# Weight loads in alternating thirds, a split first q load, and values cast on ScalarE, in a sketched-attention plus ReGLU kernel

## The chip, the core and the metric

The kernel runs on one core of a Trainium2 chip. The metric is the device time of one execution in microseconds (us); lower is better. A core has five engines that run side by side, each in its own program order: TensorE (PE, matrix multiplies; its weight loads are listed as PEld), VectorE (DVE), ScalarE (ACT), GpSimd (POOL) and SyncE (SP, which only issues DMAs here). An engine whose next instruction waits does nothing else meanwhile.

## The reference, cut to what matters

```python
# q, k, v: (4 batches, 4 heads, 1088 tokens, 32) float32;  S1, S2: (8, 32)
def phi(x):                       # 64 features of a token
    a = einsum('rd,bhsd->bhsr', S1, x)
    b = einsum('rd,bhsd->bhsr', S2, x)
    return einsum('bhsi,bhsj->bhsij', a, b).reshape(..., 64)
q_p, k_p = phi(q), phi(k)
kv = einsum('bhsf,bhsd->bhfd', k_p, v)
z = sum(k_p, axis=2)
attn = einsum('bhsf,bhfd->bhsd', q_p, kv) / (einsum('bhsf,bhf->bhs', q_p, z) + 1e-6)
x = attn.transpose(0, 2, 1, 3).reshape(4352, 128)
out = (maximum(x @ w_gate, 0) * (x @ w_val)) @ w_out     # w_gate, w_val: 128 x 1536; w_out: 1536 x 128
```

## The kernel before

**Order of work.** The whole program is unrolled, and its order is worked out in Python while it is built. Every piece of work is a `Task` with an engine, an estimated length (`occ`) and latency (`lat`), tasks that it depends on (`deps`), tasks that must merely have started (`after`) and an earliest time (`at`). `set_due` (L55) gives each task a due time, going back from the due times of the feed-forward units by latency and a slack of 200 ns for each step. `run` (L84) then puts the tasks in order: on each engine it takes, among those that can start first (within 30 ns), the one due soonest. The times in `land` (L322) are estimates of when each load has landed; a consumer is not placed earlier. The result is only an order: on the chip each engine goes through its own list, and a wrong estimate becomes a wait in which everything behind it on that engine waits too.

**Attention.** A batch has 1088 = 64 x 17 tokens, 17 columns (`c`) of 64, the first CA = 9 in partitions 0 to 63 and the other CB = 8 in partitions 64 to 127. For each batch the keys go through: two transposes of `k_sb` on DVE (L405), sketches on PE (L415), transposes back (L427), the outer product `kp` on POOL (L301; for batch 0 partly on DVE), the sum for z (L474, L486, L491, L499, ending in `wst`), and `kp` times `v_sb` on PE (L513) into `kv_bd` (L528). The queries go in groups: columns 0, 1, 2 to 3 and 4 to 7 (of each half) of batch 0, then columns 0 to 7 of batches 1, 2 and 3, then the last column of all batches. A group goes: transpose of `q_sb` (L588), PE (L612), transpose back (L627), the denominator (`bw`, `dn`, `rd`, `an`; L637 to L654), the outer product `qp` (L301; POOL from the third group on), a transposition (PE L671 and ACT L712 for batch 0; a transposing DMA on SP, L701, for batches 1 to 3), PE (L678), and an ACT cast into `xT` (L720).

**Feed-forward.** 102 units, each of 512 columns of work: gate product (PE L747 with `wg`), value product (PE L747 with `wv`), ReLU (ACT L758), their product `ht` (DVE L767) and four matmuls with `wo` that accumulate the output (PE L778). The 12 blocks `j` of 128 of the hidden dimension are split among units: a unit of the first two groups covers 4 blocks, of the third 2, then 1. After a group's units ACT copies the result out (L795) and SP stores it (L801). Up to 5 PSUM banks hold gate and value products, 14 buffers hold `ht`.

**Loads.** SP starts with S1 and the two halves of batch 0's k, then the whole of batch 0's q (L246). POOL issues the loads that cast float32 to float16 on the way: v of batch 0 (L239 and L240, two DMAs), then `wg`, `wv` and `wo` (L367, one DMA each), then v of batches 1 to 3 (two DMAs each). `fills` (L291) are four small memsets of a batch's tiles, on POOL for batches 1 to 3; the first of them stands ahead of v's load. `gate` (L393) is a POOL memset of one element of `k_sb` of batch 1: SP's load of that tile, and all of SP's loads behind it (k1, q1, k2, q2, k3, q3; L390 and L391), wait for it. Until the first unit PE runs multiplies of zeros (L824) in its idle time.

Of the kernel before, what the change touches and what calls it, by code (L numbers as in the profile page):

```python
# [9 lines left out]
FP32 = mybir.dt.float32  # L10
# [28 lines left out]
class Plan:  # L39
# [4 lines left out]
    def __init__(self, free, a_max, f_max, n_banks):  # L44
        self.tasks = []
        self.free = dict(free)
        self.a_max, self.f_max, self.n_banks = a_max, f_max, n_banks
        self.sem = 45.0

    def add(self, *args, **kw):  # L50
        t = Task(*args, **kw)
        self.tasks.append(t)
        return t

    def set_due(self, slack):  # L55
        after = {}
        for t in self.tasks:
            for d in t.deps + t.after:
                after.setdefault(id(d), []).append(t)
        order, seen = [], set()  # L60

        def visit(t):
            stack = [(t, iter(after.get(id(t), ())))]
            seen.add(id(t))
            while stack:
                top, it = stack[-1]
                for n in it:
                    if id(n) not in seen:
                        seen.add(id(n))
                        stack.append((n, iter(after.get(id(n), ()))))  # L70
                        break
                else:
                    order.append(top)
                    stack.pop()

        for t in self.tasks:
            if id(t) not in seen:
                visit(t)
        for t in order:
            for n in after.get(id(t), ()):  # L80
                s = slack if n.kind != "f" or t.kind != "f" else 0.0
                t.due = min(t.due, n.due - t.lat - s)

    def run(self, first_f):  # L84
# [97 lines left out]
def kernel(  # L182
# [12 lines left out]
    nc = tc.nc  # L195

    B, H, S, D = q.shape
# [4 lines left out]
    NJ = DF // 128  # L202
    T = 64
    C = S // T
    CA = (C + 1) // 2
    CB = C - CA
    NG = 10
    NH = 14
    assert (B, H, D, R, C) == (4, 4, 32, 8, 17)

    ctx.enter_context(tc.manual_schedule())
# [11 lines left out]
    k_sb = [const.tile([128, 2, C * D], FP32, name=f"k_sb{b}") for b in range(B)]  # L223
    q_sb = [const.tile([128, 2, (C + 1) * D], FP32, name=f"q_sb{b}") for b in range(B)]
    v_sb = [const.tile([128, H, CA * D], FP16, name=f"v_sb{b}") for b in range(B)]
    wg = const.tile([DM, NJ, 128], FP16, name="wg")
    wv = const.tile([DM, NJ, 128], FP16, name="wv")
    wo = const.tile([128, NJ, DM], FP16, name="wo")

    def load_pairs(eng, dst, src, b, hp=None):  # L230
        x = src[b].rearrange("(x y) (t c) d -> (y t) x (c d)", y=2, c=C)
        if hp is None:
            eng.dma_start(out=dst[:, :, 0:C * D], in_=x)
        else:
            eng.dma_start(out=dst[:, hp, 0:C * D], in_=x[:, hp])

    def load_v(eng, dst, b):
        x = v[b].rearrange("h (t c) d -> t h (c d)", c=C)
        eng.dma_start(out=dst[0:T], in_=x[:, :, 0:CA * D])  # L239
        eng.dma_start(out=dst[T:128, :, 0:CB * D], in_=x[:, :, CA * D:])  # L240
# [2 lines left out]
    nc.scalar.dma_start(out=s16[R:2 * R], in_=S2[:, None, :].to_broadcast([R, 4, D]))  # L243
    load_pairs(nc.sync, k_sb[0], k, 0, 0)
    load_pairs(nc.sync, k_sb[0], k, 0, 1)
    load_pairs(nc.sync, q_sb[0], q, 0)  # L246

    zero = const.tile([128, 128], FP16, name="zero")
    nc.vector.memset(zero, 0.0)  # L249
# [40 lines left out]

    def fills(eng, b):  # L291
        eng.memset(wst[b], 0.0)
        eng.memset(v_sb[b][T:128, :, CB * D:], 0.0)
        eng.memset(kt[b][:, :, C], 0.0)
        eng.memset(kv_bd[b], 0.0)

# [8 lines left out]
            op=ALU.mult,  # L305
        )

    T0, STEP, T_GATE, T_DT = 12500.0, 830.0, 12500.0, 2500.0
    P = Plan(free={"PE": 1200.0, "ACT": 3100.0, "DVE": 3600.0, "POOL": 3000.0, "SP": 20000.0},
             a_max=3, f_max=5, n_banks=7)  # L310

    def act(n):
        return dict(occ=50 + 0.835 * n, lat=175 + 0.835 * n)
# [4 lines left out]
    def pool(n):  # L318
        return dict(occ=70 + 1.86 * n, lat=120 + 1.86 * n)

    T_S = 4000.0
    land = dict(k00=4200.0, k01=4850.0, q0=6700.0, v0=8700.0, wg=10500.0, wv=13000.0, wo=16500.0,  # L322
                k1=17500.0, v1=20000.0, q1=20500.0, k2=22500.0, v2=23000.0, q2=24500.0, k3=26500.0,
                v3=26000.0, q3=28500.0)


    def e_st(t):
# [38 lines left out]
    def e_load(dst, src):  # L366
        return lambda t: nc.gpsimd.dma_start(out=dst, in_=src)  # L367

    l_v0 = P.add("ld_v0", "POOL", 1350, 1350, emit=lambda t: load_v(nc.gpsimd, v_sb[0], 0))
    l_g = P.add("ld_wg", "POOL", 740, 740, deps=[l_v0],  # L370
                emit=e_load(wg, moe_w_gate.rearrange("m (j f) -> m j f", j=NJ)))
    l_v = P.add("ld_wv", "POOL", 560, 560, deps=[l_g],
                emit=e_load(wv, moe_w_val.rearrange("m (j f) -> m j f", j=NJ)))
    l_o = P.add("ld_wo", "POOL", 1050, 1050, deps=[l_v],
                emit=e_load(wo, moe_w_out.rearrange("(j f) m -> f j m", f=128)))
    l_v_sb = [l_v0]
    l_v0.after += t_fill[:1]
    for f in t_fill[1:]:
        f.after.append(l_o)
    prev = l_o  # L380
    for b in range(1, B):
        prev = P.add(f"ld_v{b}", "POOL", 1350, 1350, deps=[prev, t_fill[b - 1]],
                     emit=lambda t, b=b: load_v(nc.gpsimd, v_sb[b], b), at=10000.0 + 3000.0 * b)
        prev.due = T0 - 1000.0 + 5000.0 * b
        l_v_sb.append(prev)

    def e_gate(t):
        nc.gpsimd.memset(k_sb[1][0:1, 0, 0:1], 0.0)
        for b in range(1, B):
            load_pairs(nc.sync, k_sb[b], k, b)  # L390
            load_pairs(nc.sync, q_sb[b], q, b)  # L391

    P.add("gate", "POOL", 70, 100, emit=e_gate, at=T_GATE).due = T_GATE  # L393


    class Keys:
# [2 lines left out]
    kk = []  # L399
    for b in range(B):  # L400
        K = Keys()
        kk.append(K)

        def ke_t1(t, b, hp):
# [100 lines left out]
        K.wst = P.add(f"k{b}wst", "DVE", **dve(32), deps=[K.w, t_w0[b]], frees=[K.z],  # L505
                      emit=lambda t, b=b, z=K.z: ke_wst(t, b, z))

        K.v = [P.add(f"v{b}", "POOL", 1, 1, deps=[l_v_sb[b]], at=land[f"v{b}"])]

        def ke_kv(t, b, lo, hi, m):  # L510
            for c in range(lo, hi):
# [55 lines left out]
    for i, (bs, c0, n, r, o0) in enumerate(groups):  # L567
        G = Group()
        gg.append(G)
        G.bs, G.c0, G.n = bs, c0, n  # L570
        X = 4 * n
        rest = len(bs) > 1
        early = i < 2
        turned = not rest and bs[0] > 0
# [22 lines left out]
        for hp in range(2) if turned else (None,):  # L597
            cost = dict(occ=560, lat=640) if rest else dve((2 if turned else 4) * n * 32, 85)
            t1.append(P.add(f"q{i}t1{hp}", "DVE", **cost, deps=free,
                            at=max(land[f"q{b}"] for b in bs),  # L600
                            emit=lambda t, G=G, hp=hp: qe_t1(t, G, hp)))

        def qe_ab(t, G):
# [89 lines left out]
        for c in range(0, n, 4):  # L693
            p = Part()
            G.parts.append(p)
            p.G, p.n, p.c0, p.col = G, min(n, 4), c, col
            col += p.n * 128
            need = phi if n <= 4 else phi[2 * (c // 4):2 * (c // 4) + 2]
            if turned:
                def qe_dt(t, G=G, c=c):  # L700
                    nc.sync.dma_start_transpose(  # L701
                        out=G.pt[:, 2 * c:2 * c + 8],
                        in_=G.qp[:, 4 * c:4 * c + 16].rearrange("s x f -> s (x f)"))

                tre = P.add(f"q{i}dt{c}", "SP", T_DT, T_DT + 1500, deps=need, after=[last_dt],
                            emit=qe_dt)
                last_dt = tre
            else:
                tr = P.add(f"q{i}tr", "PE", 58 * 2 * p.n, 58 * 2 * p.n + 170, deps=need, banks=1,
                           emit=lambda t, G=G, p=p: qe_tr(t, G, p.c0, p.n))  # L710
                tre = P.add(f"q{i}tre", "ACT", **act(256 * p.n), deps=[tr], frees=[tr],
                            emit=lambda t, G=G, f=tr, p=p: nc.scalar.copy(  # L712
                                out=G.pt[:, 2 * p.c0:2 * p.c0 + 2 * p.n].rearrange(
                                    "f x t -> f (x t)"),
                                in_=ps[:, f.bank].bitcast(FP16)[:, 0:2 * p.n * 128]))
            num = P.add(f"q{i}num{c}", "PE", 110 * p.n, 110 * p.n + 170, banks=1,
                        deps=[tre] + [kk[b].kvc for b in bs],
                        emit=lambda t, G=G, p=p: qe_num(t, G, p.c0, p.n))
            p.x = P.add(f"q{i}x{c}", "ACT", **act(128 * p.n), deps=[num], frees=[num],
                        emit=lambda t, p=p, f=num: nc.scalar.copy(  # L720
                            out=xT[:, p.col:p.col + p.n * 128], in_=ps[:, f.bank, 0:p.n * 128]))
            before.setdefault(id(r), []).append(p.x)
# [8 lines left out]
    for gi, p in enumerate(p for G in gg for p in G.parts):  # L731
# [3 lines left out]
        for i in range(NJ // per):  # L735
# [9 lines left out]
            def e_mm(t, w, p=p, js=js, W=W):  # L745
                for y, j in enumerate(js):
# [1 line left out]
                                     xT[:, p.col:p.col + W], start=True, stop=True)  # L748

            g = P.add(f"g{u}", "PE", 218, 218 + 170, deps=[p.x], banks=1, kind="f",  # L750
                      emit=lambda t, f=e_mm: f(t, wg), at=land["wg"])
            vv = P.add(f"v{u}", "PE", 218, 218 + 170, deps=[p.x, g], banks=1, kind="f",
                       emit=lambda t, f=e_mm: f(t, wv), at=land["wv"])
            g.due, vv.due = due, due + 220

            def e_relu(t, U, g):
# [53 lines left out]
                           emit=lambda t, G=G, p=p: e_evict(t, G, p))  # L810
        last_evict.due = outs[-1].due + 400

    P.set_due(200.0)
    order = P.run(T0)


# [42 lines left out]
```

## Time and profile before

| What | Value |
|---|---|
| median of 3 runs | 110.31 us (110.23 to 110.49) |
| the profiled execution | 110.49 us |
| its span, first to last instruction | 108.7 us |
| granted TensorE clock over the span | 0.993 |
| PE matmuls, busy | L747 with `wg` 35.6 us, with `wv` 36.6 us, L778 39.1 us |
| ACT, ReLU (L758) | 57.2 us, 602 ns each |
| DVE, product `ht` (L767) | 63.9 us, 676 ns each |
| HBM read and written | 9.05 MB, 2.23 MB |

Busy times of pipelined matmuls overlap, so their sum is more than the time that they hold PE; back to back, a unit's three products start 0.22 us apart each. In the timelines below, a bracket at a line's end gives the engine's idle time just before it and what ended it.

### The profile page before, as it was taken

The numbers are of one execution on the slowest core, as the hardware profiler recorded it, in microseconds if no ns is written. First come the engines' busy times: TensorE is split into PE (matmuls) and PEld (weight loads), VectorE is DVE, ScalarE is ACT, GpSimd is POOL, SyncE is SP. The second block draws the span as 40 slices with busy tenths as digits, with TensorE's granted clock in tenths as the row PEclk, the third lists the DMA queues.
The fourth block names the chain that finished last, engine by engine and source line by source line (L and its number), as shares of the span: only waits on it lengthen the run. The fifth ranks groups of instructions, "written<-read, shape, count | busy, mean of one in ns | idle before, by whom it ended". The sixth has DMA issues, their size and how long they took to land.

```text
span 108.7 us, 3081 instructions
## 1 busy us (share of the span) xinstructions
PE 99.8 (92%) x1175; PEld 66.7 (61%) x1175; DVE 91.6 (84%) x199; ACT 72.2 (66%) x140; POOL 51.1 (47%) x84
## 2 busy tenths in 40 slices
PE   6999978599999999999999999999999999999930
PEld 6778767187657554656576556565774666568710
DVE  4659973899999998999999799799995999889820
ACT  4330469168597619666978495499767989989910
POOL 6979898089829719503294088025925000000000
PEclk9999999999999999999999999999999999999997
DMA  1999999999912582100045440000471400400302
GB/s 38 319 184 158 156 221 300 309 310 311 222 31 48 103 99 54 42 0 6 0 96 113 86 96 3 0 0 11 106 148 30 103 0 0 99 1 6 82 14 48
DMA packets 14559, 10.75 MB, mean 99 GB/s; under 512 B 8657, under 2 KB 11345, under 8 KB 14545
## 3 DMA queue, kind: packets, MB, share of 16 engines
q1 hardware_dynamic: 10328, 8.20, 29.3%
q0 software_dynamic: 4016, 2.29, 15.5%
q8 instruction: 9, 0.15, 0.5%
q10 hardware_dynamic: 200, 0.07, 0.3%
q14 instruction: 6, 0.04, 0.1%
HBM read 9.05 MB, written 2.23 MB: 104 GB/s over the span
## 4 chain that ended last, share of the span: by engine, by line
PE 68%; DMA 16%; DVE 6%; POOL 3%; ACT 1%; SPq 1%; issue 1%; DVEq 1%
PE ps L747 37%; PE ps L778 18%; DMA k_sb<-in_k_dram 7%; DMA q_sb<-in_q_dram 5%; DMA pt<-qp 4%; PE ps L678 3%; PE ps L612 3%; PE ps L415 2%; POOL qp L301 2%; PE ps L474 2%; DVE kp L301 1%; ACT xT L720 1%; PE ps L513 1%; DVE abq L627 1%; DVE qt L588 1%
## 5 line engine op out<-in xcount | busy, mean ns | idle before, releaser
L758 ACT ACTIVATE g_sb<-ps 128x512 f16<-128x512 f32 x102 | 57.2, 602 | 16.3 <-PE ps L747 14.7
L767 DVE TENSOR_TENSOR ht<-g_sb,ps 128x512 f16<-128x512 f16 x102 | 63.9, 676 | 4.2 <-ACT g_sb L758 1.5
L778 PEld LDWEIGHTS <-ht 128*128 128x128 f16 x408 | 29.5, 98 | 17.8 <-DVE ht L767 4.1
L778 PE MATMUL ps<-wo,ht 128*128 128x128 f16 x408 | 39.1, 219 | 0.4 <-DVE ht L767 0.4
L747 PE MATMUL ps<-xT,wv 128*128 128x512 f16 (+2 forms) x132 | 36.6, 331 | 0.8 <-DMA wv<-in_moe_w_val_dram 0.8
L747 PE MATMUL ps<-xT,wg 128*128 128x512 f16 (+2 forms) x132 | 35.6, 330 | 0.6 <-ACT xT L720 0.5
L301 POOL TENSOR_TENSOR kp<-abk 128x640 f16<-128x640 f32 (+1 forms) x14 | 16.3, 1193 | 8.2 <-DVE abk L427 8.2
L301 POOL TENSOR_TENSOR qp<-an,abq 128x512 f16<-128x512 f32 x16 | 16.7, 1070 | 0.5
L747 PEld LDWEIGHTS <-wv 128*128 128x128 f16 x132 | 11.4, 98 | 4.6 <-issue 1.4
L747 PEld LDWEIGHTS <-wg 128*128 128x128 f16 x132 | 11.7, 98 | 3.7 <-issue 1.7
L637 POOL TENSOR_TENSOR bw<-abq 128x128 f32<-128x128 f32 (+1 forms) x9 | 3.8, 424 | 14.0 <-DVE abq L627 13.7
L720 ACT CAST xT<-ps 128x512 f16<-128x512 f32 (+2 forms) x11 | 5.4, 488 | 5.4 <-PE ps L678 5.4
L824 PE MATMUL ps<-zero 128*128 128x128 f16 x84 | 7.7, 250 | 1.1 <-DVE zero L249 1.1
L405 DVE STREAM_TRANSPOSE kt<-k_sb 128x544 f32<-128x544 f32 x8 | 5.6, 726 | 2.9 <-DMA k_sb<-in_k_dram 2.9
L654 POOL TENSOR_TENSOR an<-abq,rd 128x256 f32<-128x256 f32 (+2 forms) x6 | 2.9, 480 | 9.4 <-DVE rd L651 9.3
L824 PEld LDWEIGHTS <-zero 128*128 128x128 f16 x84 | 6.1, 113 | 1.7 <-DVE zero L249 1.1
L627 DVE STREAM_TRANSPOSE abq<-ps 128x512 f32<-128x512 f32 (+2 forms) x11 | 6.3, 577 | 0.8 <-PE ps L612 0.7
L795 ACT ACTIVATE o_sb<-ps 128x512 f32<-128x512 f32 (+2 forms) x11 | 5.5, 501 | 2.0 <-PE ps L778 1.9
L415 PE MATMUL ps<-kt,sk 64*64 64x288 f32 x64 | 5.4, 425 | 1.6 <-DVE kt L405 1.6
L678 PE MATMUL ps<-pt,kv_bd 128*128 128x512 f16 (+2 forms) x20 | 5.1, 337 | 0.3 <-DMA pt<-qp 0.2
L612 PE MATMUL ps<-qt,wst 64*64 64x256 f32 (+3 forms) x112 | 5.1, 303 | 0.0
L427 DVE STREAM_TRANSPOSE abk<-ps 128x320 f32<-128x320 f32 (+1 forms) x8 | 3.4, 460 | 1.9 <-PE ps L415 1.8
(75 smaller groups left out, 64.4 us busy)
## 6 DMA issues: line engine op xcount, KB each, us to landing
q_sb<-in_q_dram SPq DMA_DIRECT2D x4, 544.0 KB, 8.8
out_dram<-o_sb SPq DMA_DIRECT2D x14, 128.0 KB, 2.3
k_sb<-in_k_dram SPq DMA_DIRECT2D x3, 544.0 KB, 8.6
v_sb<-in_v_dram POOLq DMA_DIRECT2D x4, 144.0 KB, 8.6
k_sb<-in_k_dram SPq DMA_DIRECT2D x2, 272.0 KB, 2.7
v_sb<-in_v_dram POOLq DMA_DIRECT2D x4, 128.0 KB, 10.1
wg<-in_moe_w_gate_dram POOLq DMA_DIRECT2D x1, 384.0 KB, 7.2
wv<-in_moe_w_val_dram POOLq DMA_DIRECT2D x1, 384.0 KB, 8.5
```

What stands on the lines that cost most here:

```text
L301: eng.tensor_tensor(out=dst.rearrange("s x (i j) -> s x i j", i=R), in0=a[:, :, :, None].to_broadcast([128, n, R, R]), in1=b[:, :, None, : ...
L405: nc.vector.transpose(kt[b][:, hp, 0:C].rearrange("p c t -> p (c t)"), k_sb[b][:, hp])
L415: nc.tensor.matmul(ps[64 * st:64 * st + 64, first.bank + h2, 0:CA * 32], sk[r, 64 * hp:64 * hp + 64], kt[b][r, hp, CA * st:CA * st + CA].r ...
L612: nc.tensor.matmul(o, wst[G.bs[0]][r, hp].rearrange("p a f -> p (a f)"), G.qt[r, hp, st], start=True, stop=True, skip_group_check=True)
L627: nc.vector.transpose(G.ab[:, lo:hi].rearrange("p x h f -> p h x f"), ps[:, f.bank:f.bank + 2, lo * 32:hi * 32].rearrange("p h (x t) -> p ...
L678: nc.tensor.matmul(o, kv_bd[G.bs[0]][:, 2 * hp:2 * hp + 2].rearrange("f a d -> f (a d)"), G.ptc[:, hp, c0:c0 + n], start=hp == 0, stop=hp ...
L720: emit=lambda t, p=p, f=num: nc.scalar.copy(out=xT[:, p.col:p.col + p.n * 128], in_=ps[:, f.bank, 0:p.n * 128]))
L747: nc.tensor.matmul(ps[:, t.bank, y * W:(y + 1) * W], w[:, j], xT[:, p.col:p.col + W], start=True, stop=True)
L758: nc.scalar.activation(out=U.g_sb, in_=ps[:, g.bank], func=ACTF.Relu)
L767: nc.vector.tensor_tensor(out=U.ht, in0=U.g_sb, in1=ps[:, vv.bank], op=ALU.mult)
L778: nc.tensor.matmul(ps[:, OB, s * DM:(s + 1) * DM], U.ht[:, y * n * 128 + s * 128:y * n * 128 + (s + 1) * 128], wo[:, j], start=(j == 0 and ...
L824: nc.tensor.matmul(ps[:, OB, 0:128], zero, zero, start=True, stop=True)
```

## The change

1. `wg` and `wv` are loaded in three parts each, of 4 blocks `j`, in the order wg0, wv0, wg1, wv1, wg2, wv2; a unit's products wait only for the third that they use. The parts' due times are set by hand (2000, 2000, 8000 ns).
2. Batch 0's first q load brings only columns 0 to 3 of each half (two DMAs); the rest comes as two more DMAs, issued on SP just ahead of k1.
3. v of batches 1 to 3 comes as float32, on SP's queue after each batch's q, into new tiles `v32`, and ACT casts each in two pieces of 128 x 576 into `v_sb`.
4. All three `fills` of POOL stand behind the weight parts, and `gate` behind all three fills. Its time goes from 12500 to 10800. The load of `wo` may be issued once the weight parts have been, from 12600 on.
5. `land` is rewritten; the transposing DMA's `occ` goes from 2500 to 1700 and its `lat` from 4000 to 3500.
6. The slack becomes a task's own: 500 ns for the keys of batches 2 and 3 and the groups from the sixth on, 200 ns as before for the rest.

```diff
-    load_pairs(nc.sync, q_sb[0], q, 0)
+    load_q0(nc.sync, 0)
...
+    Q0 = 4
+    JT = NJ // 3
...
+    v32 = [const.tile([128, H, CA * D], FP32, name=f"v32_{b}") if b else None for b in range(B)]
...
+    def load_q0(eng, part):
+        x = q[0].rearrange("(x y) (t c) d -> (y t) x (c d)", y=2, c=C)
+        for st in range(2):
+            lo = (CA * st + (Q0 if part else 0)) * D
+            hi = (CA * st + (Q0 if not part else CB if st else CA)) * D
+            eng.dma_start(out=q_sb[0][:, :, lo:hi], in_=x[:, :, lo:hi])
...
-        eng.memset(v_sb[b][T:128, :, CB * D:], 0.0)
+        eng.memset((v32[b] if b else v_sb[b])[T:128, :, CB * D:], 0.0)
...
-    T0, STEP, T_GATE, T_DT = 12500.0, 830.0, 12500.0, 2500.0
+    T0, STEP, T_GATE, T_WO, T_DT, SLACK = 12500.0, 830.0, 10800.0, 12600.0, 1700.0, 500.0
...
-    land = dict(k00=4200.0, k01=4850.0, q0=6700.0, v0=8700.0, wg=10500.0, wv=13000.0, wo=16500.0,
-                k1=17500.0, v1=20000.0, q1=20500.0, k2=22500.0, v2=23000.0, q2=24500.0, k3=26500.0,
-                v3=26000.0, q3=28500.0)
+    land = dict(k00=3900.0, k01=4600.0, q0=6300.0, v0=8400.0, w0=10600.0, w1=12300.0, w2=13800.0,
+                q0b=14500.0, k1=16600.0, wo=18000.0, q1=19500.0, v1=21500.0, k2=23000.0, q2=25000.0,
+                v2=26500.0, k3=28500.0, q3=30000.0, v3=32000.0)
...
-    l_g = P.add("ld_wg", "POOL", 740, 740, deps=[l_v0],
-                emit=e_load(wg, moe_w_gate.rearrange("m (j f) -> m j f", j=NJ)))
-    l_v = P.add("ld_wv", "POOL", 560, 560, deps=[l_g],
-                emit=e_load(wv, moe_w_val.rearrange("m (j f) -> m j f", j=NJ)))
-    l_o = P.add("ld_wo", "POOL", 1050, 1050, deps=[l_v],
+    prev = l_v0
+    for y in range(3):
+        js = slice(y * JT, (y + 1) * JT)
+        for n, dst, src in (("wg", wg, moe_w_gate), ("wv", wv, moe_w_val)):
+            prev = P.add(f"ld_{n}{y}", "POOL", 570, 570, after=[prev],
+                         emit=e_load(dst[:, js], src.rearrange("m (j f) -> m j f", j=NJ)[:, js]))
+            prev.due = 2000.0 if y < 2 else 8000.0
+    for f in t_fill:
+        f.after.append(prev)
+    l_v0.due = 2000.0
+    l_o = P.add("ld_wo", "POOL", 1050, 1050, after=[prev], at=T_WO,
                 emit=e_load(wo, moe_w_out.rearrange("(j f) m -> f j m", f=128)))
-    l_v_sb = [l_v0]
-    l_v0.after += t_fill[:1]
-    for f in t_fill[1:]:
-        f.after.append(l_o)
-    prev = l_o
-    for b in range(1, B):
-        prev = P.add(f"ld_v{b}", "POOL", 1350, 1350, deps=[prev, t_fill[b - 1]],
-                     emit=lambda t, b=b: load_v(nc.gpsimd, v_sb[b], b), at=10000.0 + 3000.0 * b)
-        prev.due = T0 - 1000.0 + 5000.0 * b
-        l_v_sb.append(prev)
+    l_o.due = T_WO
 
     def e_gate(t):
         nc.gpsimd.memset(k_sb[1][0:1, 0, 0:1], 0.0)
+        load_q0(nc.sync, 1)
         for b in range(1, B):
             load_pairs(nc.sync, k_sb[b], k, b)
             load_pairs(nc.sync, q_sb[b], q, b)
-
-    P.add("gate", "POOL", 70, 100, emit=e_gate, at=T_GATE).due = T_GATE
+            load_v(nc.sync, v32[b], b)
+
+    P.add("gate", "POOL", 70, 100, emit=e_gate, at=T_GATE, after=t_fill).due = T_GATE
...
-        K.v = [P.add(f"v{b}", "POOL", 1, 1, deps=[l_v_sb[b]], at=land[f"v{b}"])]
+        if b == 0:
+            K.v = [P.add("v0", "POOL", 1, 1, deps=[l_v0], at=land["v0"])]
+        else:
+            K.v = [P.add(f"v{b}{x}", "ACT", **act(2 * CA * D), at=land[f"v{b}"], emit=lambda t, b=b, x=x:
+                         nc.scalar.copy(out=v_sb[b][:, 2 * x:2 * x + 2], in_=v32[b][:, 2 * x:2 * x + 2]))
+                   for x in range(2)]
...
-                            at=max(land[f"q{b}"] for b in bs),
+                            at=max(land["q0b" if i == 3 else f"q{b}"] for b in bs),
...
-                tre = P.add(f"q{i}dt{c}", "SP", T_DT, T_DT + 1500, deps=need, after=[last_dt],
+                tre = P.add(f"q{i}dt{c}", "SP", T_DT, T_DT + 1800, deps=need, after=[last_dt],
...
-                      emit=lambda t, f=e_mm: f(t, wg), at=land["wg"])
+                      emit=lambda t, f=e_mm: f(t, wg), at=land[f"w{max(js) // JT}"])
...
-                       emit=lambda t, f=e_mm: f(t, wv), at=land["wv"])
+                       emit=lambda t, f=e_mm: f(t, wv), at=land[f"w{max(js) // JT}"])
```

More of the change, by code (lines that the diff above doesn't have):

```diff
@@ L48, in __init__, with set_due @@
         self.sem = 45.0
+        self.slack = 200.0
     def add(self, *args, **kw):
         t = Task(*args, **kw)
+        t.slack = self.slack
         self.tasks.append(t)
         return t
-    def set_due(self, slack):
+    def set_due(self):
         after = {}
@@ L80, in set_due @@
             for n in after.get(id(t), ()):
-                s = slack if n.kind != "f" or t.kind != "f" else 0.0
+                s = t.slack if n.kind != "f" or t.kind != "f" else 0.0
                 t.due = min(t.due, n.due - t.lat - s)
@@ L401 @@
         K = Keys()
+        P.slack = 200.0 if b < 2 else SLACK
         kk.append(K)
@@ L571 @@
         X = 4 * n
+        P.slack = 200.0 if i < 5 else SLACK
         rest = len(bs) > 1
@@ L811 @@
         last_evict.due = outs[-1].due + 400
-    P.set_due(200.0)
+    P.set_due()
     order = P.run(T0)
```

## The prediction

> **What bounds the kernel now.** I read the busy shares first, then stretches of the span, then the timelines of PE, DVE and POOL where PE had gaps, and last the chain of waits.
>
> ```profile
> PE 99.8 (92%) x1175; PEld 66.7 (61%) x1175; DVE 91.6 (84%) x199; ACT 72.2 (66%) x140; POOL 51.1 (47%) x84
> ```
>
> PE is fullest, but 92% is an average. The windows of PE alone (length, busy, count, granted clock, DMA share, GB/s) show where it is not full:
>
> ```profile
> 12.80:18.60 5.80, 4.86 (x84) 1.00 1.31 244
> 18.60:20.40 1.80, 0.25 (x8) 1.00 1.13 301
> 20.40:104.60 84.20, 83.00 (x898) 1.00 0.34 77
> ```
>
> From 20.4 us to the last product PE idles 1.2 us in 84. So what can be won lies ahead of 20.4 us, and beyond it in crumbs. PE's timeline names the early gaps:
>
> ```profile
> 12.89 0.61 PE L747 MATMUL ps<-xT,wg 128*128 128x128 f16 x8
> 14.29 0.40 PE L747 MATMUL ps<-xT,wv 128*128 128x128 f16 x4 [0.79 <-DMA wv<-in_moe_w_val_dram]
> ...
> 20.35 1.34 PE L415 MATMUL ps<-kt,sk 64*64 64x288 f32 x16 [1.55 <-DVE kt L405]
> ```
>
> The first unit has its gate product and waits 0.79 us for all of `wv`; later PE waits 1.55 us for k1. Two more waits, 0.5 us together, are on casts of x (PE L747 on ACT L720). DVE had stopped for the same k1:
>
> ```profile
> 19.55 1.37 DVE L405 STREAM_TRANSPOSE kt<-k_sb 128x544 f32<-128x544 f32 x2 [2.25 <-DMA k_sb<-in_k_dram]
> ```
>
> The chain of waits (start, length) tells when that load was released and how long it took; POOL's timeline tells what released it:
>
> ```profile
> 12.45 7.08 DMA k_sb<-in_k_dram
> ```
>
> ```profile
> 9.52 1.09 POOL L367 DMA_DIRECT2D wo<-in_moe_w_out_dram  x1
> ...
> 12.34 0.09 POOL L388 MEMSET k_sb<- 1x1 f32 x1
> ```
>
> k1 goes out right behind the gate and takes 7.08 us, beside the tails of `wv` (5.75 + 8.5 = 14.2) and `wo` (9.52 + 6.9 = 16.4) and v1's cast load, which POOL issues at 12.79.
>
> ```profile
> wv<-in_moe_w_val_dram POOLq DMA_DIRECT2D x1, 384.0 KB, 8.5
> wo<-in_moe_w_out_dram POOLq DMA_DIRECT2D x1, 384.0 KB, 6.9
> ```
>
> Later PE stops briefly where a batch's first x is late:
>
> ```profile
> 39.92 0.59 PE L678 MATMUL ps<-pt,kv_bd 128*128 128x512 f16 x2 [0.24 <-DMA pt<-qp]
> ...
> 41.18 0.59 PE L747 MATMUL ps<-xT,wg 128*128 128x512 f16 x2 [0.23 <-ACT xT L720]
> ```
>
> and once more by 0.23 at 82.75. The chain from k1's landing through batch 1's keys and queries ends in that x at 40.55 to 41.13: k1's landing is paid for twice, at once at 20 and again, as a limit, at 41.
>
> **The change, part by part.** The sum is made against the profiled 110.49 (span 108.7, 1.8 around it); it stands 0.18 above the median of 110.31, so a difference is taken from the median.
>
> *POOL's queue up to the gate.* I use the durations of POOL's rows and the order that the due times give. v0's two issues (0.78 + 0.62) no longer stand behind a fill, start at 2.95 and end at 4.35. Six weight issues of 0.57 (rows of 0.58 and 0.57; a third has the same 128 rows) end at 7.8; the last two are due at 8000, ahead of batch 0's `kp`, which going back from unit 0 (12500) by the latencies and slacks is due at about 8200. `kp` (2.53) then ends at 10.3 instead of 9.57. Three fills at 0.89 (the second ran from 10.60 to 11.49) end at 13.0, and the gate comes at 13.05 instead of 12.34. By this count the later loads are released 0.7 us later, not sooner, although the gate's time was lowered: `wo` left the stretch ahead of the gate, but four weight issues and one fill entered it. `wo` is issued just behind, at 13.1 to 13.5 rather than 9.52. The later `kp` costs nothing on the path: `kv_bd` ran at 11.51 and PE used it at 12.27; without that slack it would cost 0.7.
>
> *Thirds.* Unit 0 needs the first third, which can't land later than `wg` as a whole did (5.18 + 7.2 = 12.4), and x comes at 12.6. The last third can't land later than `wv` did by much: the same bytes, issued from 4.35 to 7.8 and without `wo` behind them, so 12.4 to 14.2; unit 2 wants it at about 13.6. The wait of 0.79 falls to between 0 and 0.6, so a gain of 0.2 to 0.8; PE's queue behind it holds the second group's L671, and with it one of the waits on x. I take 0.8 for the wait and 0.2 for that x together.
>
> The Trainium skill, "DMA: Bandwidth & Descriptors", Anatomy of one DMA, speaks against thirds: it gives each POOL-issued DMA about 2.0 us fixed plus its bytes, so six in a row would be done some 8 us later than two if the fixed parts followed each other. This trace doesn't show that they do: v0's two loads, issued 0.77 us apart, landed 0.70 apart. By the rule unit 2 would stop for several us; I go by the row.
>
> *First q in two.* DVE waits only 0.30 us for q0 (L588, at 7.58), and the group's PE step waits for `wst` (8.68 to 8.85) anyway. Gain 0 to 0.3; I take 0.2. The rest of q0 stands on SP ahead of k1 and writes another tile than the gate does, so SP can issue it at once and it lands near the 7.6 of the whole q0; at worst it goes with the gate and lands at 13.05 + 0.4 + 2.6 (the shortest k row) = 16.1, for a transpose that ran at 13.35 and is now placed at 14.5: a loss of 0 to 1.6 on DVE, with products `ht` queued behind. I take 0.
>
> *k1's landing.* Release 13.05, then between 3.3 us (the two halves of k0, the same bytes: issued from 1.27, landed at 4.57, with little beside them) and 7.08 (its own row): 16.4 to 20.1. `wv` is done by then and v1 has left POOL's queue; `wo` starts later than k1. The nearer row is k0's; I take 4.2, so 17.3, 2.2 earlier than 19.53. It is placed at 16.6 on DVE, so some 0.6 us of DVE wait remain; PE's 1.55 goes: gain 1.5, between -0.6 and 1.6 by the bounds.
>
> *wo.* The output products are placed from 18.0 on PE, in order, with everything behind them. Issued at 13.3, `wo` takes between 4.1 (shortest v row) and 9.3 (median v row, beside SP's loads); its own 6.9 held a wait behind `wv`. Landing 17.4 to 22.6; I take 19.1, nearer its own row, and 0.9 us of PE wait. Bounds 0 to 4.4.
>
> *v on SP and ACT.* POOL loses three pairs of 0.68 + 0.62, 3.9 us, which held up nothing: group 3's `an` waited for DVE (`rd` 13.97, `an` 14.22). SP gains eight issues of 0.4 to 1.0; its first store (19.46) has four buffers and can wait. ACT gains six casts; the row 128x512 at 0.58 gives 0.65 for 128x576, 3.9 us in all. They are placed at the landing estimates 21.5, 26.5, 32.0, where ACT was busy 5.73 of 9.6 us, so the idle part covers them; if a v lands late, ReLUs queue behind a waiting cast and PE behind these. Bounds 0 to 3.9; I take 0.2, since five banks stand between.
>
> *Slack and the transposing DMA* change order alone. They can win the 0.24 and 0.23 at 40 and 41 and the 0.23 at 82.75, or lose a like amount at the three batch changes; -0.7 to +0.7. I take a gain of 0.2.
>
> Sum: -0.8 - 0.2 - 0.2 - 1.5 + 0.9 + 0.2 - 0.2 = -1.8; 110.3 - 1.8 = **108.5 us**, span 106.9. Lateness of k1, `wo` and v doesn't add up in full: once PE has waited, everything after it is later and the next landing less late.
>
> **Rivals.**
> *wo becomes the bound (slower).* It is issued 3.7 us later, now beside SP's loads, which have two issues of v more. The point: without the +0.9, the sum is -2.7 with first waits at 18.2, so from a landing at 20.9 on the kernel is slower. Its own row gives 20.2 and v's median 22.6: 110.3 - 2.7 + 4.4 = 112.0. For it: v1 to v3, beside SP's loads, took up to 13.3 us. Against: `wo` starts before q1 and v1 are issued. The same page of the Trainium skill (Queues, rings and completion order) says that an engine takes turns between queues by packets of some 9 to 17 descriptors; `wo`, in many small rows, would by that rule share its turns with all SP loads and land later than in my sum. No run here settles it yet.
> *k1 is not earlier (about the same).* The gate is 0.7 later and 7.08 holds: landing 20.1, batch 1's x as late as before, only `wv`'s crumbs won: 110.0, from 109.5 to 110.6. For it: the POOL count; against: what filled the DMA engines then is gone.
> *All waits go (faster still).* k1 at 16.4 and `wo` by 18: -2.7 and the batch changes' 0.7 instead of 0.2: 107.1.
>
> **How the numbers follow.** Forecast (107.5 to 109.5) 0.46; all waits gone 0.20; k1 not earlier 0.14; `wo` or a late v the bound 0.20. What can be told from no change is 0.2%, 0.22 us. Faster: 0.46 + 0.20 + 0.07; same: 0.05; slower: 0.20 + 0.02. The range goes from 106.9, a little under the third rival, to 111.2: above it lies half of the `wo` case, below it a part of the third, under 2 in 10 together. The forecast's own range is 107.5 to 109.5.
>
> **What would show it.** Right: no wait of L747 on `wv`; the gate's memset near 13.05, k1's transposes at about 17.3, batch 1's x 2 us earlier than 40.55, PE's idle ahead of 21 us down from some 3 us to 1.5. Wrong: L778 waiting for `wo` by over 2 us; L405 starting after 19; ACT waiting on `v32` with PE idle beside it; new gaps of PE behind 40 us from the other order of work.

## The result, and the profile after

| | before | changed |
|---|---|---|
| median, same chip | 110.40 us (4 runs, 110.23 to 112.22) | 123.31 us (4 runs, 122.89 to 123.64) |
| ratio | | 1.117, 95% interval 1.112 to 1.122 |
| profiled execution, its span | 110.49, 108.7 us | 123.64, 121.9 us |
| granted TensorE clock over the span | 0.993 | 0.938 |

The change makes the kernel 12% slower; 108.5 us was forecast, and 123.31 lies far above the range. Lines of the changed kernel have other numbers: L379 weight loads, L397 gate, L417 transposes of k, L427 keys on PE, L524 the casts of v, L765 gate and value products, L776 ReLU, L796 output products.

The busy line at the head of the page of the changed kernel:

```profile
PE 102.0 (84%) x1168; PEld 67.4 (55%) x1168; DVE 92.9 (76%) x199; ACT 76.3 (63%) x146; POOL 49.6 (41%) x82
```

PE has the same work and 84% instead of 92%: it waited. Its timeline shows where:

```profile
12.98 0.61 PE L765 MATMUL ps<-xT,wg 128*128 128x128 f16 x8
13.42 0.61 PE L765 MATMUL ps<-xT,wv 128*128 128x128 f16 x8
...
17.51 0.39 PE L765 MATMUL ps<-xT,wv 128*128 128x128 f16 x4
29.43 1.44 PE L796 MATMUL ps<-wo,ht 128*128 128x128 f16 x12 [11.53 <-DMA wo<-in_moe_w_out_dram]
30.67 0.63 PE L765 MATMUL ps<-xT,wg 128*128 128x256 f16 x2
31.23 2.20 PE L427 MATMUL ps<-kt,sk 64*64 64x288 f32 x16
```

The wait on `wv` is gone (13.42 follows 12.98 without a bracket), and then PE stands 11.53 us at the first output product, because `wo` isn't there. Everything behind that product on PE stands with it. DVE had batch 1's keys transposed early, and then stood as well, waiting for PE:

```profile
16.85 1.37 DVE L417 STREAM_TRANSPOSE kt<-k_sb 128x544 f32<-128x544 f32 x2 [0.34 <-DMA k_sb<-in_k_dram]
33.49 0.85 DVE L439 STREAM_TRANSPOSE abk<-ps 128x256 f32<-128x256 f32 x2 [12.50 <-PE ps L427]
```

The DMA issues (KB each, median us from issue to landing) and POOL's timeline say that `wo` was both issued later and slower:

```profile
wo<-in_moe_w_out_dram POOLq DMA_DIRECT2D x1, 384.0 KB, 16.4
```

```profile
7.57 2.60 POOL L313 TENSOR_TENSOR kp<-abk 128x640 f16<-128x640 f32 x2
...
12.67 0.09 POOL L397 MEMSET k_sb<- 1x1 f32 x1
...
12.99 1.09 POOL L379 DMA_DIRECT2D wo<-in_moe_w_out_dram  x1
```

Issued 3.47 us later than in the kernel before (9.52), landed 13.0 us later (29.39 against 16.4): the issue is a quarter of the delay, the transfer the rest, 16.4 us instead of 6.9.

The windows of PE (length, busy, count, granted clock, DMA share, GB/s) show a second loss:

```profile
17.90:21.50 3.60, 0.00 (x0) 1.00 1.32 243
21.50:29.40 7.90, 0.00 (x0) 0.50 1.16 260
29.40:35.15 5.75, 5.72 (x43) 0.50 0.98 233
35.15:117.00 81.85, 79.65 (x862) 1.00 0.23 46
```

3.6 us into the wait the granted clock falls to 0.50, and it stays there for 5.75 us after PE has work again: the 16 sketches of L427 take 2.20 us, 1.34 before. In the kernel before the clock was at 1.0 through all of this. The budget at the last output product (it begins at 116.95, before at 104.16, 12.8 later): 11.5 for `wo`; 2.9 for 5.72 us of work at half clock; 1.1 for the waits ahead of a batch's first x (0.84 and 0.96 us for `pt`, where there were 0.24, 0.23 and 0.23); less 1.55 and 0.79 for the two waits that went. That makes 13.2, 0.4 too much. PE's timeline of the changed kernel, and the last product of the kernel before:

```profile
52.30 0.59 PE L696 MATMUL ps<-pt,kv_bd 128*128 128x512 f16 x2 [0.84 <-DMA pt<-qp]
...
92.56 0.59 PE L696 MATMUL ps<-pt,kv_bd 128*128 128x512 f16 x2 [0.96 <-DMA pt<-qp]
...
116.95 0.40 PE L796 MATMUL ps<-wo,ht 128*128 128x128 f16 x4 [0.20 <-DVE ht L785]
```
```profile
104.16 0.40 PE L778 MATMUL ps<-wo,ht 128*128 128x128 f16 x4 [0.20 <-DVE ht L767]
```

*Why the transfer took so long* can be counted in the trace's own packet records. POOL's load of `wo` is 1536 records of 256 B as they land (128 partitions, 12 rows each).

```
                             before        changed
wo issued                      9.52          12.99
first, last record      11.53, 16.09  17.16, 28.31
wo records per us               336            138
SP records in that time         122           1740
```

Where v's loads (POOL) and k and q (SP) stood beside each other in the kernel before, from 19 to 27 us, 950 records of POOL and 963 of SP went out: one for one. SP's take 101 ns there (median), those of `wo` 41 ns. One for one, 16 engines do 16 / 0.142 = 113 records of `wo` a us, so all 1536 in 13.6 us, and with the 2.0 us to the first record (11.53 - 9.52) 15.6 us. Measured: 16.4. The sum agrees better than its parts: the first record came 4.2 us after the issue and not 2.0, the records took 11.15 us, and the last went out 1.1 us before the landing. All of the 15.6 stood in the trace of before.

### The profile page after: what moved, and what is told of

Same layout as the page of the kernel before. It is cut to its first block, busy times and chain, and to the rows that moved or that the text cites. A ratio compares the mean times of both kernels' runs of the same rounds, so it can differ in the third digit from the quotient of the medians.

```text
span 121.9 us, 3083 instructions
## 1 busy us (share of the span) xinstructions
PE 102.0 (84%) x1168; PEld 67.4 (55%) x1168; DVE 92.9 (76%) x199; ACT 76.3 (63%) x146; POOL 49.6 (41%) x82
## 4 chain that ended last, share of the span: by engine, by line
PE 55%; DMA 21%; POOL 14%; issue 4%; DVE 1%; DVEq 1%; ACT 0%; POOLq 0%
PE ps L765 27%; PE ps L796 16%; DMA wo<-in_moe_w_out_dram 13%; DMA pt<-qp 8%; POOL qp L313 4%; PE ps L427 3%; PE ps L630 3%; PE ps L696 2%; POOL kp L313 2%; PE ps L486 2%; POOL wg L379 1%; POOL wv L379 1%; POOL an L672 1%; DVEq L872 1%; POOL v_sb L251 1%
## 5 line engine op out<-in xcount | busy, mean ns | idle before, releaser
L785 DVE TENSOR_TENSOR ht<-g_sb,ps 128x512 f16<-128x512 f16 x102 | 65.0, 675 | 5.7 <-PE ps L765 3.0
L776 ACT ACTIVATE g_sb<-ps 128x512 f16<-128x512 f32 x102 | 58.4, 600 | 15.1 <-PE ps L765 12.6
L796 PE MATMUL ps<-wo,ht 128*128 128x128 f16 x408 | 39.8, 224 | 11.9 <-DMA wo<-in_moe_w_out_dram 11.5
L796 PEld LDWEIGHTS <-ht 128*128 128x128 f16 x408 | 30.1, 100 | 31.4 <-issue 13.7
L765 PE MATMUL ps<-xT,wv 128*128 128x512 f16 (+2 forms) x132 | 37.5, 333 | 0.0
L765 PE MATMUL ps<-xT,wg 128*128 128x512 f16 (+2 forms) x132 | 36.7, 335 | 0.1
L765 PEld LDWEIGHTS <-wg 128*128 128x128 f16 x132 | 11.9, 99 | 2.8 <-issue 0.7
L765 PEld LDWEIGHTS <-wv 128*128 128x128 f16 x132 | 11.8, 99 | 2.1 <-issue 0.4
L417 DVE STREAM_TRANSPOSE kt<-k_sb 128x544 f32<-128x544 f32 x8 | 5.8, 736 | 1.2 <-DMA k_sb<-in_k_dram 1.2
L427 PE MATMUL ps<-kt,sk 64*64 64x288 f32 x64 | 6.4, 495 | 0.0
## 6 DMA issues: line engine op xcount, KB each, us to landing
v<-in_v_dram SPq DMA_DIRECT2D x3, 256.0 KB, 13.2
```

Of the source, the lines that this page charges most:

```text
L417: nc.vector.transpose(kt[b][:, hp, 0:C].rearrange("p c t -> p (c t)"), k_sb[b][:, hp])
L427: nc.tensor.matmul(ps[64 * st:64 * st + 64, first.bank + h2, 0:CA * 32], sk[r, 64 * hp:64 * hp + 64], kt[b][r, hp, CA * st:CA * st + CA].r ...
L765: nc.tensor.matmul(ps[:, t.bank, y * W:(y + 1) * W], w[:, j], xT[:, p.col:p.col + W], start=True, stop=True)
L776: nc.scalar.activation(out=U.g_sb, in_=ps[:, g.bank], func=ACTF.Relu)
L785: nc.vector.tensor_tensor(out=U.ht, in0=U.g_sb, in1=ps[:, vv.bank], op=ALU.mult)
L796: nc.tensor.matmul(ps[:, OB, s * DM:(s + 1) * DM], U.ht[:, y * n * 128 + s * 128:y * n * 128 + (s + 1) * 128], wo[:, j], start=(j == 0 and ...
```

## The experiments

Theory from here on: `wo`, in many small rows, is late because it starts behind the gate, where SP's loads share the DMA engines with it; the wait then costs the clock as well. Rivals: v on SP's queue is what did it; the clock is beside the point; another part of the change costs as much by itself. Medians and ratios are against runs of the kernel before on the same chip.

**`wo` issued ahead of the fills (the changed kernel).**
```diff
-    l_o = P.add("ld_wo", "POOL", 1050, 1050, after=[prev], at=T_WO,
+    l_o = P.add("ld_wo", "POOL", 1050, 1050, after=[prev],
...
-    l_o.due = T_WO
+    l_o.due = 8100.0
```


> The changed kernel with one edit: wo is issued right behind batch 0's kp and ahead of the fills, as in the kernel before, so at about 10.1 us instead of 12.99; the gate comes 1.1 us later. Theory A (wo, 1536 small rows, takes turns with SP's loads and so lands at 29.39): wo is nearly done when SP's loads start, lands at 15 to 17, PE's first L796 does not wait, the clock stays at 1.00, and the kernel takes 107.5 to 109.5 us. Rival B (splitting the weights has clogged POOL's DMA queue, whoever else loads): wo still takes over 12 us, the kernel over 115 us. Rival C (the other edits cost as well: casts on ACT, new order of work): no wait for wo, but 110.5 us or more.

115.27 us, ratio 1.044 (1.038 to 1.050): 8.0 of the 12.9 us come back. `wo` is issued at 10.04 and lands at 16.78, and PE waits for it no more. So the theory holds for `wo`, but not for the time of 107.5 to 109.5 us: rival C, that the other edits cost as well, holds too. DVE's, PE's and ACT's timelines:

```profile
20.98 1.37 DVE L417 STREAM_TRANSPOSE kt<-k_sb 128x544 f32<-128x544 f32 x2 [4.01 <-DMA k_sb<-in_k_dram]
```
```profile
21.87 2.20 PE L427 MATMUL ps<-kt,sk 64*64 64x288 f32 x16 [3.58 <-DVE kt L417]
33.82 0.38 PE L765 MATMUL ps<-xT,wg 128*128 128x512 f16 x1 [1.20 <-ACT g_sb L776]
34.88 0.38 PE L765 MATMUL ps<-xT,wv 128*128 128x512 f16 x1 [0.46 <-ACT g_sb L776]
```
```profile
32.60 0.67 ACT L524 CAST v_sb<-v 128x576 f16<-128x576 f32 x1 [2.04 <-DMA v<-in_v_dram]
```

k1, issued at 13.83, is transposed only at 20.98, and a late v2 stops ACT, and through the ReLUs behind it PE. Both had been hidden under the wait for `wo`. PE's 3.58 us again brought 3.4 us at half clock (21.5 to 24.9).

**`wo` in 128 rows of 6144 B instead of 1536 of 512 B (the changed kernel).**
```diff
-                emit=e_load(wo, moe_w_out.rearrange("(j f) m -> f j m", f=128)))
+                emit=e_load(wo, moe_w_out.rearrange("(f j) m -> f j m", j=NJ)))
```


> The changed kernel with wo loaded as 128 rows of 6144 bytes instead of 1536 rows of 512: same bytes, same place and time of issue (12.99). This pairs the hidden units with other rows of w_out than the reference does; all instructions and their order are the same. Theory A (turns are taken by rows, not by bytes): wo lands at 16.5 to 20 and the kernel takes 107.5 to 111 us. Rival D (POOL's queue gets a small share of the bytes, or comes last): wo still lands after 25 us, the kernel takes over 118 us.

This kernel leaves out the right pairing of hidden units and rows of `w_out`, so its output is another one. 115.97 us (2 runs), ratio 1.051 (1.043 to 1.058). The same bytes on the same queue beside the same SP loads:

```profile
wo<-in_moe_w_out_dram POOLq DMA_DIRECT2D x1, 384.0 KB, 8.6
```
```profile
22.69 1.13 PE L796 MATMUL ps<-wo,ht 128*128 128x128 f16 x12 [3.38 <-DMA wo<-in_moe_w_out_dram]
```

8.6 us instead of 16.4 for the same bytes: about half of the price beside SP's loads was the number of rows. It is less than expected: `wo` landed at 22.65, not by 20. Its first record still went out 3.4 us after the issue.

**SP's loads behind k1 held until `wo` has landed (the changed kernel).** A POOL copy of one element of `wo` into `q_sb` of batch 1 holds them.
```diff
+    def e_gate2(t):
+        nc.gpsimd.tensor_copy(out=q_sb[1][0:1, 0, 0:1], in_=wo[0:1, 0, 0:1])
...
+    P.add("gate2", "POOL", 70, 100, emit=e_gate2, at=15700.0, after=[l_o]).due = 15700.0
```


> The changed kernel with SP's loads behind k1 (q1, v1 and all later ones) held back by a one-element POOL copy that waits for wo's landing; wo is issued at the same 12.99 with its small rows, beside k1 alone. Theory A: wo lands at 17.5 to 19.5, PE waits for it 2 us at most, q1 lands 3 us later than its estimate of 19.5, and the kernel takes 109 to 112 us. Rival E (wo is slow because it is issued late and its rows are small, with or without SP's loads): it lands after 24 us, the kernel over 117 us.

116.78 us (2 runs), ratio 1.058 (1.048 to 1.068). With only k1 on SP's queue `wo` takes 6.6 us, and its first record goes out 2.1 us after the issue. The company on the engines is the other half of the cause. The time of 109 to 112 us was missed all the same: v1 lands at 28.3, ACT waits 3.87 us for it, and PE 3.28 us on an output copy queued behind. In the profiled execution everything also starts 2.1 us later (the last section tells of such starts), so `wo` was issued at 14.28 and landed at 20.85.

**Zeros multiplied through the wait (the changed kernel).**
```diff
+        if t.name == "out0":
+            for _ in range(190):
+                nc.tensor.matmul(ps[:, OB, 0:128], zero, zero, start=True, stop=True)
```


> The changed kernel with 190 products of zeros (56 ns each, 10.6 us) on PE ahead of the first L796, where PE waits for wo. Nothing else changes; wo lands at 29.4 as before. If the half clock that the profile shows from 21.5 to 35.15 us costs time of its own, it stays at 1.00 and the kernel is 2.0 to 2.8 us faster than the changed kernel (120.5 to 121.3 us). If the half clock is hidden behind other waits, the time stays within 0.5 us of 123.3.

118.84 us (four runs: 117.92, 117.97, 119.70, 122.24), ratio 1.077 (1.065 to 1.088): 4.5 us less than the changed kernel by the medians, 5.4 by the two lowest runs, by more work. That is more than the 2.0 to 2.8 us expected. Its windows of PE:

```profile
17.70:27.90 10.20, 10.20 (x187) 1.00 1.23 254
27.90:33.60 5.70, 5.70 (x90) 1.00 1.07 246
33.60:111.00 77.40, 77.19 (x827) 1.00 0.27 53
```

The clock stays at 1.00, and 90 products fit where the changed kernel did 43. `wo` landed 1.5 us earlier in this execution (27.87), which the zeros don't explain, and the first output product came 1.1 us sooner (28.34). From it to the last it is 82.9 us instead of 87.5: 4.6 less. Of these 2.9 are the half clock; the rest is the two later waits for `pt`, which are gone here. That the zeros removed them as well isn't shown.

**v back on POOL, `wo` left late (the changed kernel).**
```diff
+        prev = P.add(f"ld_v{b}", "POOL", 1350, 1350, deps=[prev, t_fill[b - 1]],
+                     emit=lambda t, b=b: load_v(nc.gpsimd, v_sb[b], b), at=10000.0 + 3000.0 * b)
...
-            load_v(nc.sync, v32[b], b)
```


> The changed kernel with v of batches 1 to 3 back on POOL as cast loads behind wo; wo stays late (issued near 13), k and q of three batches stay on SP beside it. Theory 'wo in small rows shares its turns with whatever stands on SP's queue': the six k and q loads behind the gate are enough, wo lands between 22 and 28, PE waits 4 to 10 us for it, the granted clock falls to 0.5 behind that, 115 to 121 us. Rival 'it is v's eight issues on SP that make wo late': wo lands by 20, PE waits under 2 us, the clock stays at 1.0, 110.5 to 112.5 us.

121.71 us, ratio 1.107 (1.097 to 1.116). The rival falls: six k and q loads on SP are enough; `wo` lands at 28.35.

```profile
28.39 1.44 PE L796 MATMUL ps<-wo,ht 128*128 128x128 f16 x12 [10.18 <-DMA wo<-in_moe_w_out_dram]
```

**Both: `wo` early and v back on POOL.**


> Run e1 (wo early) with v of batches 1 to 3 taken back to POOL's cast loads, issued after wo as in the kernel before; no casts on ACT, SP loads k and q only. If v's move is what is left of e1's loss (theory H): 111 to 113 us. If the loss sits in k1 (e1: DVE waits 4.0 us for k1, PE 3.6): k1 still lands near 21 and the kernel takes 113 to 115 us.

110.70 us (10 runs: six from 109.97 to 110.81, four from 113.42 to 114.55); the ratio, of the six, is 1.007 (1.003 to 1.011). By the ratios, each on its own chip, that is some 4.0 us less than with `wo` early alone. This is what v on SP and ACT costs once `wo` no longer hides it, as far as the six speak for the kernel: the profile is of one of them (109.97), and what the other four met isn't known.

```profile
17.79 1.37 DVE L422 STREAM_TRANSPOSE kt<-k_sb 128x544 f32<-128x544 f32 x2 [0.84 <-DMA k_sb<-in_k_dram]
```

k1 takes 4.0 us here, issued at 13.80, and the clock stays at 1.0. So with both undone the thirds, the q in two, the fills' new place and the slack are left, and they come to nothing or a little worse.

**`wo` early, v on SP behind all k and q.**
```diff
+        for b in range(1, B):
             load_v(nc.sync, v32[b], b)
```


> The changed kernel with wo issued behind kp (115.3 us, k1's transposes at 20.98), and on SP the three v loads behind all k and q loads. Theory 'k1 is late because v1 stands on the same queue close behind it and takes its turns': k1's transposes at 17.5 to 18.5, PE's wait for them under 1 us; the v loads then land 4 to 6 us later and ACT waits for them from 25 us on, 113 to 116 us. Rival 'k1 is late for another reason (wo's tail, the gate at 13.7)': k1's transposes stay at 20 or later, and ACT's waits come on top, 116 to 119 us.

120.90 us, ratio 1.098 (1.090 to 1.106), slower than both theories said. DVE and ACT:

```profile
18.48 1.37 DVE L418 STREAM_TRANSPOSE kt<-k_sb 128x544 f32<-128x544 f32 x2 [0.18 <-DMA k_sb<-in_k_dram]
```
```profile
30.45 0.67 ACT L525 CAST v_sb<-v 128x576 f16<-128x576 f32 x1 [7.85 <-DMA v<-in_v_dram]
```

k1, issued at 14.46, is there at 18.48: 4.0 us instead of 7.15, so v1 close behind had delayed it. But it isn't the only condition: in the changed kernel v1 stood just as close and k1 took 4.1 us; only with `wo`'s tail still draining was it 7.15. How the two act together stays open. The size of the loss was missed because ACT's cast has a fixed place in its queue: a v 5 us later (30.4) stopped ACT for 7.85 us and PE for 7.6, and the clock was at half for 10.2 us from 26.3 on.

**Parts of the change alone, on the kernel before.** Thirds only, with no other part:


> The kernel before with the weights in alternating thirds and nothing else (one fill still ahead of v0, wo still behind kp, v still on POOL). Theory F (four more issues on POOL push everything behind them: kp, wo, fills, gate): the wait on wv goes, but the gate comes at 13.8 to 14.2 us instead of 12.34, k1 lands after 20.5 and DVE waits longer for it; 110.6 to 113 us. Rival G (the thirds are worth their 0.8 us by themselves, and what is lost elsewhere is lost to other parts of the change): 109.0 to 110.0 us.

114.23 us median, but the four runs go from 110.50 to 120.77. The wait on `wv` goes, as theory F said, but the gate came sooner (11.95, before 12.34) and not later. In the profiled run `wo` was issued at 10.87, the gate came ahead of its drain, and PE waited 2.94 us for it (9.4 us from issue):

```profile
20.30 0.58 PE L781 MATMUL ps<-wo,ht 128*128 128x128 f16 x4 [2.94 <-DMA wo<-in_moe_w_out_dram]
```

From 19.14 to 25.97 the clock was at half. Six issues instead of two push `wo` toward the gate; how much that costs changes from run to run, so no price follows.

v on SP with the casts only:


> The kernel before with v of batches 1 to 3 as float32 on SP's queue behind each q and cast on ACT, and the changed kernel's landing estimates from q1 on; weights whole, wo and gate where they were (9.5, 12.3). Theory H (the casts are placed at landing estimates that SP's queue does not keep, and ReLUs wait behind a waiting cast, as run e1 shows with 2.0 us): ACT waits for v between 21 and 35 us by 1 to 3 us, PE behind it; 110.8 to 113 us. Rival I (without POOL's v loads beside it k1 lands earlier, and ACT has room): 109.0 to 110.4 us.

115.02 us median, but one of the four runs took 111.15, the others 114.32 to 116.42. ACT's timeline of the slower kind (115.71) has the price:

```profile
26.89 0.67 ACT L507 CAST v_sb<-v 128x576 f16<-128x576 f32 x1 [2.78 <-DMA v<-in_v_dram]
...
34.45 0.67 ACT L507 CAST v_sb<-v 128x576 f16<-128x576 f32 x1 [3.06 <-DMA v<-in_v_dram]
```

The first of these stops PE for 1.84 us (at 28.11), and from 29.31 to 32.73 the clock is at half.

Slack and estimates of the transposing DMA only:


> The kernel before with the slack of 500 for late batches and the new occ and lat of the transposing DMA, and nothing else: only the order of work after 33 us can change. Theory J (order alone, small): 109.8 to 110.8 us. Rival K (the waits of 0.6 to 1.2 us on the transposing DMA at two batch changes, which the changed kernel and e1 show, come from this part): 111 to 113 us, with PE waiting for pt at the batch changes by over 0.8 us.

108.40 us (107.53 to 109.27), ratio 0.984 (0.977 to 0.991): below the kernel before, by less than 2%, and better than either theory said. Its PE timeline, first gate product and last output product:

```profile
12.99 0.38 PE L751 MATMUL ps<-xT,wg 128*128 128x128 f16 x4
...
102.92 0.40 PE L782 MATMUL ps<-wo,ht 128*128 128x128 f16 x4 [0.20 <-DVE ht L771]
```

The same two stood at 12.89 and 104.16 before: 89.9 us between them instead of 91.3. Ahead of k1's sketches the loads' landings differ from one execution to the next, so the stretch behind them is the better measure: from the sketches' start (19.60, before 20.35) to the last output product 83.3 us instead of 83.8. PE does wait for `pt` at two batch changes, 0.69 and 0.28 us, so what rival K named is there; the kernel is faster all the same.

The slack only:


> The kernel before with the slack of 500 for late batches alone; the estimates of the transposing DMA stay at 2500 and +1500. Theory 'the slack makes batch 2's and 3's first x earlier': 108.0 to 108.8, x of the third batch near 58.8. Rival 'it is the estimates that order the transposing DMA': 109.7 to 110.5, x of the third batch near 61.2.

109.25 us (107.57 to 109.88), ratio 0.984 (0.972 to 0.996), between the two forecasts, and 82.5 us from the sketches (20.70) to the last output product (103.23). PE's timeline from 30 to 100 us names no wait at all; those of 0.24, 0.23 and 0.23 are gone, and the waits for `pt` with the new estimates don't come. The first x of the third batch stands at 60.03, between the two as well, but counted from the sketches it comes after 39.3 us: 40.9 before, 39.2 with slack and estimates. So the slack alone is enough.

Slack, estimates and q in two loads:


> The kernel before with the slack of 500 for the late batches and the other estimates of the transposing DMA (108.4 in the run of that part alone), and batch 0's q in two loads, both issued at once on SP. Theory 'the parts that move no load in the crowded stretch from 12 to 30 us keep their small gains': 108.0 to 108.6, a ratio of 0.98 to 0.988. Rival 'the gain of the slack was a run that came out well': 109.5 to 110.3.

109.74 us (12 runs), ratio 0.996 (0.992 to 1.0003): no difference that this measurement settles, and inside the rival's range. From the sketches (21.14) to the last product (104.26) it is 83.1 us, less than the 83.8 of before as in the other two kernels (0.5 to 1.3 us less, one execution each), so a small gain of the slack is likely, not shown. In the profiled execution, one of the slower ones (110.97), the first gate product comes at 14.54. The clock's late start (last section) goes with that; the split q alone doesn't bring it, since the changed kernel has it too and starts at 12.98.

## Why the prediction was wrong

It was wrong in the sign, and the step that failed is **"*wo.*"**: landing 19.1, bounds 17.4 to 22.6, 0.9 us of PE wait with bounds 0 to 4.4. It landed at 29.39 and PE waited 11.53. The bounds came from latencies of other loads (4.1 and 9.3, v's shortest and median), where the number of rows counts: each of v's two DMAs has 256 of them (64 tokens, 4 heads) where `wo` has 1536. "`wo` starts before q1 and v1 are issued" was no argument either: its first record came at 17.16, when q1, v1, k2 and q2 were queued.

The rival "`wo` becomes the bound" was the right mechanism at the wrong price: 112.0 for a landing at 22.6. The page it cited, the Trainium skill's "DMA: Bandwidth & Descriptors" (Queues, rings and completion order), says that queues share an engine by turns; the counts above agree (950 and 963 records), and by such turns the landing comes to 12.99 + 15.6 = 28.6. The text called the question open where the trace of before could price it. And the price for 22.6 was short too: with long rows `wo` landed at 22.65 and the time was 115.97. PE waited 3.38 us, less than the 4.4 priced, but 3.4 us at half clock (worth 1.7) and 1.6 us of later waits for `pt` came on top, and in the profiled execution a start 1.8 us later.

**The clock** was missing altogether. A wait of PE was priced at its length. It cost more here: 5.72 us of work at half clock, worth 2.9, and the run with zeros is 4.5 us faster by the medians, some of it by an earlier landing. The Trainium skill, "TensorE: Matmul & The Clock Gate", Part 1, has the rule: the clock is halved after an idle window of about 3.4 us and restored after a busy one. The traces agree on the length: half clock from 21.5 to 35.15 is 13.65 us, four times 3.41, and with `wo` early it lasted 3.41. They don't agree that a whole window must be idle. Lay each trace out in steps of 3.41 us from the first record of its granted clock: in the fourteen profiles half clock follows every step in which PE idled 1.78 us or more, and none with 1.71 or less. The steps nearest the edge:

```
                              PE idle, us   clock after it
thirds only, from 15.73           1.78      half
SP's loads held, from 27.22       2.12      half
v on SP only, from 25.90          2.20      half
the slack only, from 17.43        1.71      full
wo early, from 31.72              1.66      full
before, from 18.39                1.55      full
```

So about half a step of idle was enough, and the kernel before stood close to it. (The ends of products are modelled in the trace, so the edge is known to some 0.1 us at best.) From half clock a step with 0.45 us idle brought the full clock back, one with 1.10 didn't.

The other steps:
- *POOL's queue*: right. `kp` ended at 10.17 (10.3), the gate came at 12.67 (13.05), `wo` was issued at 12.99 (13.1 to 13.5). "The later loads are released later, not sooner" holds.
- *Thirds*: right on the wait and on the rule weighed against it; the six parts landed at 9.45 to 12.67, about 0.64 us apart, not 2.0.
- *First q in two*: the rest was issued at once and landed at 8.58; the first gate product came at 12.98 instead of 12.89, so of the 0.2 nothing.
- *k1's landing*: right. Forecast 17.3, transposed from 16.85, with `wo` starting later, as the text argued. But its 1.5 us were worth nothing while PE stood at `wo`.
- *v on SP and ACT*: the casts' 0.65 us was right (0.66 to 0.68), the sum's term wrong. 0.2 was taken, of bounds 0 to 3.9; it is some 4.0 us behind an early `wo` (ratios 1.044 and 1.007), and on the kernel before anything from 1.2 to 6.5 (four runs, against 109.9). SP gained nine issues, three of q and six of v, not eight. What "five banks stand between" left out: a cast stands in order in ACT's queue, at an estimated landing, and fp32 v doubles what POOL's cast loads had to write.
- *Slack and the transposing DMA*: right in sign, mis-sized. 0.2 was taken, up to 0.7. By the medians it is 1.5 us with the estimates (109.9 and 108.4) and 1.4 without (110.61 and 109.25), but with the split q no difference is clear; single profiles show 0.5 to 1.3 behind k1. Three visible waits of 0.23 were taken for all there was to win.

## What to carry to other kernels

A load is priced by its rows, and by who is queued beside it when its first row goes out: count the rows that pass in a stretch where two queues run together, and don't carry over a latency from a quiet stretch or from a load with fewer rows. In a kernel whose order is fixed, the transfer that the next in-order instruction needs belongs ahead of a gate that releases many megabytes, and a wait removed elsewhere is worth nothing behind it. A wait of TensorE is to be priced with the half clock that may follow: here 1.78 us of idle in 3.41 were enough.

## What was not expected of the hardware

Executions differ in when PE reaches full clock at the start. Windows of PE of the changed kernel and of the one with `wo` in long rows, which are the same program up to there:

```profile
5.50:7.00 1.50, 1.50 (x24) 1.00 1.20 203
7.00:8.50 1.50, 1.50 (x33) 1.00 1.33 210
```
```profile
5.50:7.00 1.50, 1.50 (x16) 1.00 1.22 221
7.00:8.50 1.50, 1.50 (x19) 1.00 1.31 219
```

Between 7.0 and 8.5 us 19 products start in the second and 33 in the first, and its first gate product comes at 14.77 instead of 12.98. The view gives the granted clock as 1.00 in both, but it has no record of it there: the trace's first record, with which the full clock begins, stands at 4.43 us in the first and at 9.41 in the second. Six of the fourteen profiled executions look like the second (first record at 8.54 to 10.16, first gate product at 14.54 to 15.03); in the other eight the record stands at 3.77 to 4.91. So 1.6 to 2.1 us of a time can be this, and a median over few runs carries it. What sets it no run here shows.
